# Reordering the opening of a one-core attention and gated-convolution kernel, with some of its steps on other engines

## The chip, the cores and the metric

The kernel runs on one core of one Trainium2 chip. The metric is device time in microseconds of one execution. Before the change the median of three runs was 580.38 us (580.14 to 581.49).

## What is computed

The reference is windowed attention with a linear distance bias, followed by a feed-forward block with a width-3 convolution as gate. Everything is float32.

```python
# attention: q, k, v are (8, 8, 576, 64); window 128
scores = scale * np.matmul(q, k.transpose(0, 1, 3, 2))
...
mask = (rel >= 0) & (rel < window)
scores = np.where(mask, scores + bias[None], -1000000000.0)
scores = scores - np.max(scores, axis=-1, keepdims=True)
attn = np.exp(scores)
attn = attn / (np.sum(attn, axis=-1, keepdims=True) + 1e-09)
return np.matmul(attn, v)
...
# feed-forward: x is (8, 576, 512), d_ff 1024, three taps along the sequence
h = np.maximum(x @ w_in, 0.0)
for k in range(K):
    conv_out += conv_w[k][None, None, :] * hp[:, k:k + S, :]
gate = 1.0 / (1.0 + np.exp(-conv_out))
return (h * gate) @ w_out
```

## The kernel before

The 8 x 576 tokens are 36 tiles of 128 (t = 0 to 35). Each tile's eight heads are handled as two halves u of four heads. The feed-forward block works on chunks of two tiles, in four steps of 256 hidden features each, so step s belongs to chunk s // 4. Most matmuls run on numbers that are split into a rounded high part and a low remainder, as three products: high by high, low by high, high by low.

The work is written as **pieces**. A piece is a name with numbers, and `emit` calls the function behind it; each engine runs its instructions in the order in which the pieces stand in three strings: `OPENING` (592 pieces: tiles 0 to 10, steps 0 to 10 in part, and the preparation of all weights), `PERIOD` (two tiles and four steps, repeated 14 times) and `TAIL`. An engine never overtakes: an instruction that waits holds up all that stand behind it on its engine, and on SP, which issues the DMAs, a DMA that waits for a free buffer holds up the next DMAs. The PSUM pool `pst` has five banks that are shared by all transposes, scores, attention products and up-projections.

The pieces that the text speaks of, with their engine:

- weights: `F` fetches block b (SP, L164; blocks 0 to 3 and 5 to 8 are w_in, 4 the taps, 9 to 16 w_out), `CL` clamps it (POOL, L171), `RP`/`RS` rescales its upper words (`w_rebias`: POOL L182 or ScalarE L184), `SG` keeps their sign alone (POOL, L188), `V` puts the bits together (DVE, two instructions, L203 or L207 and L210), `H` rounds to the high part (ACT, L216), `W` forms the low half (`w_lo`, L229: POOL for the blocks in `LOW_POOL`, else DVE).
- attention of tile t, half u: `QU` transposes q and k (PE, L324), `QV` copies them out (ACT, L330); from tile 9 on `TQ` (DVE, L342), `HQ` (ACT, L355) and `LQ` (POOL, L361) do this in their place; `S` scores (PE, L424, from tile 9 on L380), `MP` and `MB` mask and bias (DVE, L450 and L468), `X` exponentials (ACT, L476), `NR` reciprocals of the sums (L487 ACT, L488 DVE), `N` scales the rows by them (`normal`, L495: DVE for t < 8, else POOL) and `NA` the same on ACT in four instructions (`normal_act`, L501); `T` transposes (PE, L508), `RL` copies out (ACT, L513), `SEL` masks (POOL, L519 and L522), `AV` multiplies by v (PE, L626), `XH` and `XL` split the result into `ring`, the input of the feed-forward block (ACT L645, DVE L654), `XF` copies an edge (DVE, L660).
- feed-forward step s: `UH` up-projection (PE: L687 plain float32 for s < 4, L692 three products after), `HH` relu (ACT, L700 and L704), `Z` middle tap (ACT, L710), `CA` and `CB` outer taps (DVE, L725), `TH` tanh (ACT, L732), `GT` gate (DVE, L740), `GH` high part (ACT, L752), `GL` low half (`g_lo`, POOL, L760) and a copy of an edge (POOL, L761, or L756 for s < 4), `D` down-projection (PE, L784 for s < 4, L794 after), `OB` copies out and stores (ACT L810, then SP).

An up-projection of chunk 2 (`UH8`, `UH9`) needs `XL5` and `XL6`, which stand on DVE; a down-projection `D4` and later needs `GL` of its step and `W` of its two blocks.

Of the kernel before, what the change touches and what calls it, by code (L numbers as in the profile page):

```python
# [22 lines left out]
def tile_alibi_window_attention_conv_glu(  # L23
# [847 lines left out]
    X5.0.1 HH3.0 CA1.0 CB1.0 Z1.1 V12 XH3 XH4 CA1.1 UH3.1 QU7.1 NR5 NA5.1 T5.1 CB1.1 TH1 XL4 XL3 XF4 W3 W2 UH4.0
    UH5.0 QV7.1 GT1 RS9 SG9 Z2.0 LD9 HH2.1 QM7.1 RS11 HH3.1 CA2.0 CB2.0 Z2.1 KT6.0 X6.0.0 W6 RS13 UH4.1 CA2.1 HH4
    CB2.1 V9 S7.1 MP7.1.1 GL1 TH2 CL14 GT2 MP7.1.0 QU7.0 QV7.0 QM7.0 X6.0.1 SG13 Z3.0 X6.1.1 X6.1.0 CA3.0 LD12 CB3.0
    Z3.1 N6.0 UH5.1 D0 SG11 W7 UH7.0 RL5.1 T6.0 MB7.1.1 NA5.0 CL16 CA3.1 CB3.1 TH3 HH5 W10 T5.0 UH7.1 V11 GT3 RS16
    GL3 SEL5.1 RL5.0 MB7.1.0 H11 V13 Z4.0 CA4.0 S7.0 CB4.0 HH7 Z4.1 N6.1 MP7.0.0 GL2 CA4.1 SG16 MB7.0.0 SEL5.0 RL6.0
# [62 lines left out]
```

## Time and profile before

| | |
|---|---|
| median of three runs | 580.38 us (580.14 to 581.49) |
| profiled execution, its own time | 581.25 us |
| span of its instructions | 579.5 us |
| busy: PE, DVE, ACT, POOL | 562.4, 466.7, 434.2, 395.4 us |
| matmul instructions | 6121 |
| share of PE in the chain that ended last | 78% |

The profile is of one execution. A line's busy time is the time in which its instructions ran; "idle before" is the time in which the engine had nothing running just before them, with what ended it behind an arrow. The page's second part cuts the span into 40 slices of 14.5 us and gives the busy tenths of each engine and the clock that PE was granted. A busy PE is not PE at its peak, as matmuls are pipelined and their ends modelled; the distance from one group's start to the next one's says more.

### The profile page before, as it was taken

Reading aid. Unit: us, or ns where it says so; the run is one execution under the profiler, and the core shown is the slowest. Engines: PE = TensorE matmul, PEld = TensorE weight load, DVE = VectorE, ACT = ScalarE, POOL = GpSimd, SP = SyncE. Lnnn points to the kernel's source line nnn. Section 1 sums busy time; section 2 is a strip of 40 time slices with the busy share of each in tenths; the row PEclk is TensorE's granted clock in tenths of the full one; section 3 lists DMA queues with packets and bytes.
Section 4 is the critical chain, followed back from the end, with each engine's and each line's share of the span. In section 5 each row is a group of like instructions: output and inputs, shape, how many; then the busy total and the mean of one; then the engine's idle time right before and its main releaser. Section 6 shows DMA issues by size and latency. Waiting matters only on the chain.

```text
span 579.5 us, 16999 instructions
## 1 busy us (share of the span) xinstructions
PE 562.4 (97%) x6121; PEld 491.2 (85%) x6121; DVE 466.7 (81%) x1472; ACT 434.2 (75%) x1235; POOL 395.4 (68%) x451
## 2 busy tenths in 40 slices
PE   8898999799999999999999999999999999999997
PEld 7576886589898989898989898989898989899996
DVE  7798989898888987798778887788888987775444
...
PEclk9999999899999999999999999999999999999999
...
GB/s 191 259 228 198 138 98 57 42 108 124 167 128 162 123 162 132 158 137 161 134 162 131 164 133 170 127 172 122 171 121 168 126 166 82 146 110 18 21 3 73
DMA packets 141225, 76.63 MB, mean 132 GB/s; under 512 B 116412, under 2 KB 131028, under 8 KB 141140
## 3 DMA queue, kind: packets, MB, share of 16 engines
...
## 4 chain that ended last, share of the span: by engine, by line
PE 78%; DVE 10%; ACT 5%; DMA 2%; issue 2%; SPq 2%; POOL 1%; DVEq 0%; ACTq 0%; POOLq 0%
PE p L692 31%; PE o L794 31%; PE sc L380 7%; PE av L586 6%; DVE zp L725 2%; DVE sc L450 2%; DVE e L468 1%; ACT e L476 1%; DMA wst<-in_moe_w_in_dram 1%; DVE wg L210 1%; PE av L626 1%; SPq L164 1%; DMA rqk<-in_k_dram 1%; SPq L314 1%; DVE wst L203 1%
## 5 line engine op out<-in xcount | busy, mean ns | idle before, releaser
L692 PE MATMUL p<-ring,wi 128*128 128x256 f32 x1088 | 197.0, 283 | 3.0 <-DVE ring L654 3.0
L725 DVE SCALAR_TENSOR_TENSOR zp<-hh,cw,zp 128x256 f32<-128x256 f32 (+7 forms) x384 | 160.5, 418 | 41.3 <-ACT zp L710 34.2
L692 PEld LDWEIGHTS p<-ring,wi 128*128 128x128 f32 x1088 | 169.8, 189 | 7.4 <-issue 4.0
L692 PE MATMUL p<-ring,wl 128*128 128x256 f32 x544 | 152.9, 281 | 0.0
L760 POOL TENSOR_TENSOR gl<-z,gh 128x512 fp32r<-128x512 f32 x67 | 86.9, 1297 | 77.5 <-ACT gh L752 76.8
L476 ACT ACTIVATE e<-e,st 128x128 f32<-128x128 f32 x288 | 112.9, 394 | 18.3 <-DVE st L468 17.9
L794 PE MATMUL o<-wo,gh 128*128 128x512 f32 x270 | 110.3, 409 | 0.0
L794 PE MATMUL o<-wo,gl 128*128 128x512 f32 x270 | 105.8, 392 | 0.0
L794 PE MATMUL o<-wl,gh 128*128 128x512 f32 x270 | 105.6, 391 | 0.0
L692 PEld LDWEIGHTS p<-ring,wl 128*128 128x128 f32 x544 | 103.4, 190 | 0.0
L710 ACT ACTIVATE zp<-hh,cw 128x256 f32<-128x256 f32 x144 | 68.9, 479 | 30.4 <-DVE z L740 21.8
L361 POOL TENSOR_TENSOR qkT_low<-blk,qkT 128x1024 fp32r<-128x1024 f32 x27 | 65.1, 2411 | 16.9 <-ACT qkT L355 11.2
L495 POOL TENSOR_TENSOR e<-e,st 128x512 f32<-128x512 f32 x56 | 58.3, 1041 | 21.0 <-DVE st L488 20.1
L468 DVE CUSTOM_DVE_ANT_0 e<-sc,bias 128x128 f32<-128x128 f32 x288 | 69.2, 285 | 2.1 <-DVE sc L450 0.7
L732 ACT ACTIVATE zp<-zp 128x512 f32<-128x512 f32 (+1 forms) x73 | 42.1, 577 | 35.7 <-DVE zp L725 35.7
L794 PEld LDWEIGHTS o<-wo,gh 128*128 128x128 f32 x270 | 50.6, 187 | 13.7 <-issue 0.2
L794 PEld LDWEIGHTS o<-wo,gl 128*128 128x128 f32 x270 | 50.6, 187 | 12.0 <-POOL gl L760 0.4
L740 DVE SCALAR_TENSOR_TENSOR z<-zp,hh 128x512 f32<-128x512 f32 (+1 forms) x73 | 49.3, 675 | 13.5 <-ACT zp L732 11.6
L704 ACT ACTIVATE hh<-p 128x512 f32<-128x512 f32 x67 | 40.0, 597 | 25.2 <-PE p L692 25.0
L794 PEld LDWEIGHTS o<-wl,gh 128*128 128x128 f32 x270 | 50.8, 188 | 9.5
L450 DVE COPY_PREDICATED sc<-m_prev,sc 128x256 f32<-128x256 uint8 x128 | 51.1, 420 | 6.7 <-PE sc L380 6.7
L476 ACT ACTIVATION_READ_ACCUMULATOR e<-e,st 128x1 f32 x288 | 54.3, 189 | 0.0
...
## 6 DMA issues: line engine op xcount, KB each, us to landing
...
rr<-scr SPq DMA_DIRECT2D x112, 128.0 KB
...
rqk<-in_q_dram SPq DMA_DIRECT2D x216, 32.0 KB
rqk<-in_k_dram SPq DMA_DIRECT2D x216, 32.0 KB
...
```

The lines of the kernel that those rows point to most:

```text
L361: nc.gpsimd.tensor_tensor(out=turned_of(qkT_low, t), in0=blks[t], in1=hi, op=ALU.subtract)
L450: nc.vector.copy_predicated(out=s_cur, mask=mask.unsqueeze(1).to_broadcast(shp), data=data)
L468: nc.vector.tensor_tensor_reduce(out=e[:, j, :], in0=s_cur[:, g, :], in1=bias[:, head_of(t, u * HU + j), :], scale=-0.125, scalar=FAR, op0 ...
L476: nc.scalar.activation(out=e[:, j, :], in_=e[:, j, :], func=AF.Exp, bias=st[:, 0, j : j + 1], scale=-1.0, accum_out=st[:, 1, j : j + 1],)
L495: eng.tensor_tensor(out=e, in0=e, in1=st[:, 2, :].unsqueeze(2).to_broadcast([P, HU, P]), op=ALU.mult)
L692: nc.tensor.matmul(ps, a[:, part], ring[:, i, cc, cols], start=cc == 0 and n == 0, stop=cc == NCC - 1 and n == 2)
L710: nc.scalar.activation(out=zps[s][:, ff, :], in_=hhs[s][:, ff, 1 : 1 + CW], func=AF.Copy, scale=cw[:, 1, f : f + 1])
L725: nc.vector.scalar_tensor_tensor(out=z[:, ff, a:cut], in0=hh[:, ff, a + kk : cut + kk], scalar=cw[:, kk, f : f + 1], in1=z[:, ff, a:cut], ...
L732: nc.scalar.activation(out=zps[s][:, ff], in_=zps[s][:, ff], func=AF.Tanh)
L740: nc.vector.scalar_tensor_tensor(out=zgs[s][:, ff], in0=zps[s][:, ff], scalar=1.0, in1=hhs[s][:, ff, 1 : 1 + CW], op0=ALU.add, op1=ALU.mult,)
L760: nc.gpsimd.tensor_tensor(out=gl, in0=zgs.pop(s), in1=as32(gh), op=ALU.subtract)
L794: nc.tensor.matmul(to, a[:, ff, ms], w[:, part], start=first and n == 0, stop=end and n == 2)
```

## The change

Only the string `OPENING` and the rules for who does four kinds of step in it change. The first 54 pieces stay, some 100 more are nearly as before, and from piece 160 on the order is another one; the same pieces are done, each once. `PERIOD` and `TAIL` are as they were.

- Scaling the rows (`N`; `NA` is gone): (2,1) and (3,1) go from ACT to DVE, (6,0) from DVE to POOL, (7,0) and (7,1) from DVE to ACT.
- Low halves of the weights (`W`): 0, 1, 5 and 12 go from POOL to DVE, 6, 8 and 11 from DVE to POOL.
- Rescaling of the weights (`RS`; `RP` is gone): 3 and 8 go from POOL to ACT, 1, 7 and 11 from ACT to POOL.
- Low halves of the gate (`GL`): 4 and 7 go from POOL to DVE. The copies of the edge stay on POOL.

The two sets `KL_POOL` and `LQ_DVE` are empty.

```diff
-    LOW_POOL = {0, 1, 2, 3, 5, 7, 9, 10, 12, 13, 14, 15, 16}
+    LOW_POOL = {2, 3, 6, 7, 8, 9, 10, 11, 13, 14, 15, 16}
+    RB_POOL = {0, 1, 2, 5, 6, 7, 11}
+    N_ACT = {(1, 0), (2, 0), (3, 0), (4, 0), (4, 1), (5, 0), (5, 1), (7, 0), (7, 1)}
+    N_POOL = {(6, 0), (8, 0), (8, 1), (9, 0), (9, 1), (10, 0), (10, 1)}
+    GL_DVE = {4, 7}
+    KL_POOL = set()
+    LQ_DVE = set()
...
-    def w_rebias(b, pool=False):
+    def w_rebias(b):
...
-        if pool:
+        if b in RB_POOL:
             nc.gpsimd.tensor_scalar(out=g, in0=hf, scalar1=2.0**-112, scalar2=1.0, op0=ALU.mult, op1=ALU.mult)
...
-        eng = nc.vector if t < FIRST else nc.gpsimd
+        es[t, u] = e
+        if (t, u) in N_ACT:
+            for j in range(HU):
+                nc.scalar.activation(out=e[:, j, :], in_=e[:, j, :], func=AF.Copy, scale=st[:, 2, j : j + 1])
+            return
+        eng = nc.gpsimd if t > TURN + 1 or (t, u) in N_POOL else nc.vector
         eng.tensor_tensor(out=e, in0=e, in1=st[:, 2, :].unsqueeze(2).to_broadcast([P, HU, P]), op=ALU.mult)
...
-            nc.gpsimd.tensor_tensor(out=gl, in0=zgs.pop(s), in1=as32(gh), op=ALU.subtract)
+            eng = nc.vector if s in GL_DVE else nc.gpsimd
+            eng.tensor_tensor(out=gl, in0=zgs.pop(s), in1=as32(gh), op=ALU.subtract)
...
     OPENING = """
...
-    RS15 SG15 V15 W16 XL6 D2 HQ9 GH5 H12 Z6.0 MP8.0.0 LQ9 H15 CA6.0 GL5 CB6.0 MB8.0.0 LD10 X7.1.1 GH4 MP8.1.0 W13
...
+    MP8.1.0 TH5 GT5 D2 XH6 XL6 UH9.0 X8.0.0 MP8.1.1 Z6.0 CA6.0 CB6.0 GH4 H14 LD12 N7.0 T7.0 SG15 W10 W13 MP8.0.1 TQ9
+    W14 Z6.1 MB8.1.1 HQ9 UH8.0 V15 GH5 GL5 UH9.1 N7.1 CA6.1 CB6.1 TH6 UH8.1 H15 RL7.0 HH9 MB8.1.0 LD11 LV8 MB8.0.1
```

The order of the instructions shows the change at three places. (Line numbers of the changed kernel are 6 or so higher.) The first is DVE around `XL6`, the row that writes `ring` from `av6`, and `V15`, the two rows on `wst15` and `wg15`. Before:

```order
L654 TENSOR_TENSOR ring_126<-av5_1319,ring_126 128x4x128
L725 SCALAR_TENSOR_TENSOR zp5_1291<-hh1_132,cw_121,zp5_1291 128x256
L342 STREAM_TRANSPOSE blk_1390<-rqk9_1001 128x4x4x2x32
L740 SCALAR_TENSOR_TENSOR z5_1393<-zp5_1291,hh1_132 128x512
L203 SCALAR_TENSOR_TENSOR wst15_848<-wst15_848 128x512
L210 SCALAR_TENSOR_TENSOR wg15_1395<-wg15_1395,wst15_848 128x512
L654 TENSOR_TENSOR ring_126<-av6_1336,ring_126 128x4x128
```

Changed:

```order
L746 SCALAR_TENSOR_TENSOR z5_1394<-zp5_1293,hh1_132 128x512
L660 TENSOR_TENSOR ring_126<-av6_1326,ring_126 128x4x128
L458 COPY_PREDICATED sc8_1_1_1377<-m_prev_94,sc8_1_1_1377 128x2x128
L731 SCALAR_TENSOR_TENSOR zp6_1418<-hh2_133,cw_121,zp6_1418 128x256 x2
L496 RECIPROCAL st7_0_1213<-st7_0_1213 128x4
L458 COPY_PREDICATED sc8_0_1_1358<-m_prev_94,sc8_0_1_1358 128x2x128
L348 STREAM_TRANSPOSE blk_1460<-rqk9_890 128x4x4x2x32
L476 ISA e8_1_1390,st8_1_1391<-sc8_1_1_1377,bias_110 128x128
...
L209 SCALAR_TENSOR_TENSOR wst15_1033<-wst15_1033 128x512
L216 SCALAR_TENSOR_TENSOR wg15_1281<-wg15_1281,wst15_1033 128x512
```

`V15` and the transpose of tile 9 (`TQ9`) stood ahead of `XL6` and now stand behind it.

The second is ACT around `OB3`, the two copies to `ob0`, which wait for the down-projection `D3`, and the reciprocal sums of (8,0), the row that writes `st8_0` from itself. Before:

```order
L476 ACTIVATE e8_0_1414,st8_0_1415<-e8_0_1414,st8_0_1415 128x128 x2
L810 COPY ob0_0_1541<-o0_0_1124 128x512
L810 COPY ob0_1_1544<-o0_1_1125 128x512
L487 ACTIVATE st8_0_1415<-st8_0_1415 128x4
L710 ACTIVATE zp7_1522<-hh3_134,cw_121 128x256
```

Changed:

```order
L495 ACTIVATE st8_0_1372<-st8_0_1372 128x4
L716 ACTIVATE zp7_1552<-hh3_134,cw_121 128x256
L710 ACTIVATE hh0_131<-p8_1468 128x2x256
L817 COPY ob0_0_1632<-o0_0_1093 128x512
L817 COPY ob0_1_1635<-o0_1_1094 128x512
L758 CAST gh6_1638<-z6_1554 128x512
L738 ACTIVATE zp7_1552<-zp7_1552 128x512
```

The sums of (8,0) come ahead of the two copies; a high part and a tanh now stand behind them.

The third is DVE ahead of `V6`, the row that reads `wst6`, early in the opening. Before:

```order
L203 SCALAR_TENSOR_TENSOR wst10_420<-wst10_420 128x512
L210 SCALAR_TENSOR_TENSOR wg10_676<-wg10_676,wst10_420 128x512
L488 RECIPROCAL st4_501<-st4_501 128x8
L203 SCALAR_TENSOR_TENSOR low6_767<-wst6_465 128x512
L210 SCALAR_TENSOR_TENSOR wg6_742<-wg6_742,low6_767 128x512
```

Changed (the row of `V6` stands ten rows further down):

```order
L209 SCALAR_TENSOR_TENSOR wst10_420<-wst10_420 128x512
L216 SCALAR_TENSOR_TENSOR wg10_679<-wg10_679,wst10_420 128x512
L458 COPY_PREDICATED sc5_1_0_625<-m_prev_94,sc5_1_0_625 128x2x128
L458 COPY_PREDICATED sc5_1_0_625<-m_after_102,neg_90 128x2x128
L235 TENSOR_TENSOR wl5_725<-wg5_556,wi_119 128x512
L458 COPY_PREDICATED sc5_0_1_730<-m_prev_94,sc5_0_1_730 128x2x128
```

`W5` and one half of the mask and bias of (5,0) have come ahead of `V6`, as `W0`, `N2.1` and `N3.1` have further up.

## Rows read from the trace of the kernel before

**Rows 1.** The page's second part: busy tenths of PE and its granted clock.

```profile
PE   8898999799999999999999999999999999999997
...
PEclk9999999899999999999999999999999999999999
```

**Rows 2.** Windows: length, busy us of PE, PEld, DVE, ACT, POOL; clock, DMA, GB/s.

```profile
20.00:60.00 40.00, 35.80 (x261) 27.16 (x262) 35.95 (x119) 37.95 (x128) 31.76 (x43) 1.00 0.85 205
60.00:107.00 47.00, 41.49 (x344) 32.26 (x343) 43.54 (x96) 36.28 (x101) 28.49 (x33) 0.99 0.40 100
107.00:147.00 40.00, 39.26 (x367) 32.58 (x366) 33.05 (x111) 29.03 (x94) 27.09 (x31) 0.96 0.29 90
...
175.00:204.00 29.00, 29.00 (x369) 26.07 (x368) 26.79 (x89) 21.80 (x64) 21.92 (x25) 1.00 0.62 143
```

**Rows 3.** Waits from 20 to 147 us: who waited for whom, us, times, longest.

```profile
DVE st L488 <- ACT st L487: 7.0, 7, 2.8
...
PE p L692 <- DVE ring L654: 3.0, 1, 3.0
```

**Rows 4.** DVE in order of time, around XL6: start, us, what, idle before.

```profile
99.32 1.24 DVE L342 STREAM_TRANSPOSE blk<-rqk 128x1024 f32<-128x1024 f32 x1
...
101.40 1.75 DVE L203 SCALAR_TENSOR_TENSOR wst<-wst 128x512 uint32<-128x512 uint32 x1 [0.27 <-POOL wst L188]
103.25 2.64 DVE L210 SCALAR_TENSOR_TENSOR wg<-wg,wst 128x512 uint32<-128x512 uint32 x1
105.82 0.68 DVE L654 TENSOR_TENSOR ring<-av,ring 128x512 fp32r<-128x512 f32 x1
```

**Rows 5.** POOL in order of time in the same stretch.

```profile
102.56 2.79 POOL L361 TENSOR_TENSOR qkT_low<-blk,qkT 128x1024 fp32r<-128x1024 f32 x1
```

**Rows 6.** Windows of PE alone: length, busy us, granted clock, DMA.

```profile
105.00:106.00 1.00, 0.00 (x0) 1.00 0.29 65
...
107.00:108.00 1.00, 1.00 (x6) 0.50 0.33 73
```

**Rows 7.** The chain that ended last, in order of time: start, us, what.

```profile
40.65 6.17 DMA wst<-in_moe_w_in_dram
...
106.64 5.96 PE p L692 x36
...
151.81 5.69 PE p L692 x48
```

**Rows 8.** Single lines, 15 to 147 us: ns as shortest, median, longest.

```profile
L229 DVE TENSOR_TENSOR wl<-wg,wi x2: 686/1014/1341, 58.8 to 71.5; 128x512 fp32r<-128x512 f32 x2
L229 DVE TENSOR_TENSOR wl<-wg,wo x1: 1429/1429/1429, 118.5 to 118.5; 128x512 fp32r<-128x512 f32 x1
...
L495 DVE TENSOR_TENSOR e<-e,st x7: 684/693/1918, 14.5 to 120.9; 128x512 f32<-128x512 f32 x7
...
L760 POOL TENSOR_TENSOR gl<-z,gh x6: 1282/1292/1714, 105.3 to 142.3; 128x512 fp32r<-128x512 f32 x6
...
L501 ACT ACTIVATE e<-e,st x36: 385/394/414, 18.6 to 80.2; 128x128 f32<-128x128 f32 x36
```

**Rows 9.** DVE in order of time, early and late in the opening.

```profile
50.52 1.12 DVE L203 SCALAR_TENSOR_TENSOR low<-wst 128x512 uint32<-128x512 uint32 x1 [1.16 <-POOL wst L188]
...
116.79 0.18 DVE L488 RECIPROCAL st<-st 128x4 f32<-128x4 f32 x1 [2.81 <-ACT st L487]
...
120.92 1.92 DVE L495 TENSOR_TENSOR e<-e,st 128x512 f32<-128x512 f32 x1
```

**Rows 10.** ACT in order of time: the second of the two copies of OB3.

```profile
116.07 0.59 ACT L810 COPY ob<-o 128x512 f32<-128x512 f32 x1 [1.13 <-PE o L784]
```

**Rows 11.** PE in order of time: AV6, the first scores of tile 9 and of tile 11.

```profile
96.55 1.09 PE L626 MATMUL av<-rl,rv 128*64 128x128 f32 x16 [0.35 <-POOL rl L522]
...
117.83 0.33 PE L380 MATMUL sc<-qkT 32*128 32x128 f32 x4
...
147.16 0.38 PE L380 MATMUL sc<-qkT 32*128 32x256 f32 x1 [0.82 <-DVE ring L654]
```

More of the change, by code (lines that the diff above doesn't have):

```diff
@@ L871, in tile_alibi_window_attention_conv_glu @@
[L871 to L875, printed above, removed]
@@ L876, in tile_alibi_window_attention_conv_glu @@
-    UH6.0 RS14 H9 UH6.1 HH6 Q8 W9 CB4.1 SEL6.0 X7.0.0 SH14 V14 TH4 GT4 V16 H14 W14 Z5.0 CA5.0 MP7.0.1 QO8 CB5.0 T6.1
-    RL6.1 SEL6.1 QL8 H13 Z5.1 CA5.1 H16 D1 MB7.0.1 AV5 AV6 XH5 X7.1.0 XL5 S8.1 XH6 S8.0 CL15 LV7 CB5.1 TQ9 TH5 GT5
-    RS15 SG15 V15 W16 XL6 D2 HQ9 GH5 H12 Z6.0 MP8.0.0 LQ9 H15 CA6.0 GL5 CB6.0 MB8.0.0 LD10 X7.1.1 GH4 MP8.1.0 W13
-    MP8.0.1 Z6.1 UH9.0 W12 UH9.1 X7.0.1 UH8.0 CA6.1 D3 CB6.1 TH6 N7.0 T7.0 X8.0.0 LV9 GT6 MB8.1.0 MB8.0.1 HH9 Z7.0
-    CA7.0 UH8.1 MP8.1.1 CB7.0 X8.0.1 OB3 N8.0 MB8.1.1 TQ10 W11 Z7.1 CA7.1 CB7.1 RL7.0 N7.1 GL4 S9.0 TE8.0 HQ10 LQ10
@@ L881, in tile_alibi_window_attention_conv_glu @@
[L881 to L884 removed]
+    X0.0.0 RS0 MP0.1.0 MB0.1.0 QU1.1 QV1.0 I2 S1.0 SG0 F3 QV1.1 MP0.1.1 MB0.1.1 X0.0.1 MP1.0.1 MB1.0.1 I2 S1.1 I2
@@ new lines, in tile_alibi_window_attention_conv_glu @@
+    X5.1.0 HH0.1 LD7 MP5.0.0 MB5.0.0 UH2.0 QV6.1 UH3.0 KH6.1 KL6.1 Z0.0 CA0.0 RL4.1 SEL3.0 MP6.0.0 CB0.0 S6.1 CL12
+    SEL4.0 H3 SEL3.1 AV3 MP6.0.1 H2 RS12 SG12 Z0.1 MB6.0.0 X5.0.0 SEL4.1 AV4 W1 HH2.0 CA0.1 CB0.1 MP6.1.0 CL9 MB6.1.0
+    KL6.0 MB6.0.1 HH3.0 X5.0.1 H7 LD9 TH0 NR5 GT0 XH3 X6.1.0 V12 Z1.0 CA1.0 CB1.0 UH3.1 GL0 XH4 UH2.1 XL4 F13 KT6.0
+    RS9 MP6.1.1 N5.1 XL3 W2 Z1.1 CA1.1 CB1.1 XF4 H6 SG9 HH3.1 H8 MB6.1.1 TH1 GT1 QU7.1 QV7.1 W3 QU7.0 QM7.1 Z2.0
+    HH2.1 CA2.0 T5.1 CB2.0 W8 RL5.1 CL11 RS11 KT6.1 SG11 F16 V9 CL13 Z2.1 CA2.1 CB2.1 UH4.0 CL16 X6.1.1 X6.0.0 QV7.0
@@ new lines, in tile_alibi_window_attention_conv_glu @@
+    MP8.1.0 TH5 GT5 D2 XH6 XL6 UH9.0 X8.0.0 MP8.1.1 Z6.0 CA6.0 CB6.0 GH4 H14 LD12 N7.0 T7.0 SG15 W10 W13 MP8.0.1 TQ9
+    W14 Z6.1 MB8.1.1 HQ9 UH8.0 V15 GH5 GL5 UH9.1 N7.1 CA6.1 CB6.1 TH6 UH8.1 H15 RL7.0 HH9 MB8.1.0 LD11 LV8 MB8.0.1
+    X8.0.1 TQ10 Z7.0 GT6 X8.1.0 LQ9 D3 CA7.0 CB7.0 W16 GL4 N8.0 Z7.1 HH8 W12 CA7.1 S9.0 MP9.1.0 OB3 GH6 GL6 CB7.1 TH7
+    MP9.1.1 MB9.1.1 X8.1.1 GT7 MP9.0.1 TE8.0 T7.1 RL7.1 MB9.0.1 Z8.0 N8.1 CA8.0 CB8.0 HQ10 LQ10 MP9.0.0 Z8.1 W15
+    SEL7.0 TE8.1 WE8 X9.0.1 D4 D5 D6 CA8.1 CB8.1 TH8 GT8 GH7 SEL7.1 MB9.0.0 X9.0.0 MB9.1.0 GL7 N9.0 UH10.1 Z9.0 CA9.0
@@ L885, in tile_alibi_window_attention_conv_glu @@
+    GH8 GL8 CB9.0 S10.0 D7 MP10.1.0 MB10.1.0 MP10.1.1 X9.1.0 MB10.1.1 X9.1.1 N9.1 Z9.1 X10.1.0 X10.1.1 TE9.0 SE8
+    CE8.1 CA9.1 CB9.1 TH9 MP10.0.0 GT9 UH10.0 N10.1 CE8.0 TE9.1 MP10.0.1 LV9 WE9 OB7
     """
```

49 lines of the change are left out of this document (21 added, 28 removed).

## The prediction, made before the changed kernel ran

> **What bounds the kernel now.** I began with the slices of the page [rows 1]. PE shows sevens and eights in the first eight slices (116 us) and nines after them, and its clock is granted in full but for a slice or two there. The windows say the same in microseconds [rows 2]: in the period PE is busy 29.00 of 29.00, and the nines go on to the tail. As the period and the tail keep their order, time can be won or lost only by when PE gets through the opening. There it is busy 35.80 of 40, 41.49 of 47 and 39.26 of 40 us [rows 2]: 10.4 us idle, of which the middle window has most.
>
> DVE is the engine beside it. It is busy 35.95, 43.54 and 33.05 us in the three windows [rows 2], so 14.5 us idle, and the list of waits puts 7.0 us of that down to reciprocals that wait for a sum from ACT [rows 3]. The longest wait of PE itself is one of 3.0 us, an up-projection that waits for a row of `ring`, a DVE instruction [rows 3].
>
> The order of time shows why. XL6, 0.68 us, starts at 105.82, directly behind the two instructions of V15, which ran 1.75 and 2.64 us [rows 4]. Other such instructions take 0.69 us when nothing stands against them (W on DVE, same size, shortest 686 ns) [rows 8]. Beside V15 POOL ran LQ9, from 102.56 for 2.79 us [rows 5]. So V15 cost 4.39 where 1.38 would do. PE stood still meanwhile, and when it went on its granted clock was 0.50, the lower of its two levels (1.2 of 2.4 GHz) [rows 6]. The 36 matmuls that came then took 5.96 us; 48 at full clock take 5.69, so 36 would take 4.27 [rows 7]. That is 1.7 us on top of the 3.0.
>
> At the very end of the opening PE waits again for DVE, 0.82 us before the scores of tile 11 [rows 11]. So neither engine leads by much, and I keep an account for each. The later of the two sets the time.
>
> **The change in PE's account.** XL6 now stands in front of V15 and TQ9 (first pair of order rows). Its wait of 3.0 goes, and with it the 1.7 at the low clock: -4.7 us. What is late next is the down-projection D2 ahead of it on PE, so nothing more comes of it. The select that held AV6 for 0.35 [rows 11] stands earlier on POOL: -0.35.
>
> Against this, V6 comes later on DVE. In front of it now stand N2.1, N3.1, W0 and W5, 0.69 each [rows 8], 2.8 us, and half of the mask and bias of (5,0), which is then missing further down and so makes no difference at XF4, where UH4 waits. V6 waited 1.16 us for POOL [rows 9], which swallows part. What POOL waited for was block 6, 6.17 us on its way after V5 gave a buffer free [rows 7]; V5 is late by the first three of these, 2.1, so block 6 lands later too, but V6 is later by more. What is left at XF4 is 2.8 - 1.2 = +1.6 (between V6 and XF4 W8 leaves DVE and W1 comes). Its ends are 0, if PE has slack there, and 2.8.
>
> PE: -4.7 - 0.35 + 1.6 = **-3.5 us**.
>
> **The change in DVE's account.** By the sets, DVE loses one N and gains one W and two GL, net two instructions of 0.69: +1.4. (GL on DVE is not in the trace; W has the same operands, two from SBUF and one float32r out, so I take 0.69, and 1.43, W's longest [rows 8], as the upper end.)
>
> V15 no longer meets LQ9, whose input TQ9 and HQ9 make later; POOL has W10, W13, W14 there. Free it would save 3.0; if both halves take 1.43, as W11 did, 1.5. I take 1.5, since POOL's queue is not empty there.
>
> N7.1 took 1.92 [rows 9], W11 1.43 and W8 1.34 [rows 8]; all three leave DVE, and what they took over 0.69 is 1.2 + 0.7 + 0.7 = 2.6. New on DVE are N2.1, N3.1, W0, W1, W5, W12, GL4 and GL7. The ten N and W of the trace were stretched by these 2.6 in all, 0.26 each; eight times that is 2.1. Net -0.5.
>
> N8.0's reciprocal waited 2.81 us on DVE [rows 9]: its sum stood on ACT behind the two copies of OB3, the second of which ran at 116.07 after waiting for PE [rows 10]. Now the sum is ahead of them (second pair of order rows). But a tanh is now behind them, and DVE soon needs the scores of tile 9, which PE makes after the same D3. I take half, 1.4, between 0 and 2.8. And V6's 1.16 goes: -1.2.
>
> DVE: +1.4 - 1.5 - 0.5 - 1.4 - 1.2 = **-3.2 us**.
>
> The other moves cost nothing by these rows. Two N (7,0 and 7,1) add 4 x 0.39 us each on ACT [rows 8], as two (2,1 and 3,1) leave it. ACT loses one rescaling. POOL gets it and one N for two GL of 1.29 [rows 8] and one W, and is idle 8 to 18 us in each window [rows 2]. On SP, F13 now stands behind the 16 issues of LD9, and LV9 behind SE8; block 13 is wanted by D6 and v of tile 9 in the period, and the DMA share of the last two windows is 0.40 and 0.29 [rows 2], so neither is late by these rows. If ACT's cover were gone, T7.0 would wait for N7.0, at most its 1.6 us.
>
> The smaller gain rules: -3.2. The profiled execution took 581.25 us (579.5 of span and 1.75 around it) and would take 578.05. It lies 0.87 above the median of the runs shown, so I forecast 580.38 - 3.2 = **577.2 us**.
>
> **A rule that speaks against it.** The trace shows one DVE instruction of V15 at 2.64 us with LQ9 beside it, and N and W between 0.69 and 1.92 [rows 4, 5, 8]. The Trainium skill, page "SBUF — State Buffer", section "Who interferes with whom", says that a DVE instruction with two SBUF inputs and a GpSimd instruction that reads SBUF exclude each other, the later one blocked until the first has ended. These rows agree with it, and by it each of the eight instructions new on DVE is exposed. If each stood behind a whole instruction like GL, 1.29 [rows 8], they would lose 10.3 us, and DVE's sum would be +5.0; by the mean of the rows it is -3.2.
>
> **The rivals.**
>
> *Slower: the moved instructions are blocked by POOL.* Place: GL4 and W12 beside LQ9, W16 and the N of tile 8; W0, W1, W5 beside the selects and weights of the first 60 us. Price: if each of the eight loses what N7.1 lost, 1.23, DVE has 9.8 in place of 2.1: -3.2 + 7.7 = +4.5, **584.9 us**; at 1.0 each 583. It decides from 0.66 each on, where the gain is gone. For it speaks V15; against it that most of the old ones ran nearly free: N's shortest is 684 ns and its median 693 [rows 8]. Chance 0.22.
>
> *No change: the wait moves to the scores of tile 9.* LQ9 ended at 105.35 and these scores began at 117.83 [rows 5, 11], 12.5 us of cover. Now TQ9 (1.24) [rows 4], a copy on ACT, GL5 (1.29) [rows 8] and LQ9 (2.79) come one after another behind XL6, some 6 us, and three W on POOL, taken like GL, may come between: up to 10. PE has two up-projections (48 matmuls, 5.69 [rows 7]) and D3, which has no row here, to cover it. If POOL is 2 to 3 us late, PE idles again, and the low clock with its 1.7 can come again: 577.2 + 1.5 + 1.7 = **580.4 us**. Chance 0.21.
>
> *More: both accounts at their good ends.* Without the early lag PE has -4.7 - 0.35, and without the 0.82 wait at the end -5.9; DVE would allow it (V15 free, the whole 2.81 saved: -6.1). **574.5 us**. Chance 0.12.
>
> **How the numbers follow.** The forecast, between 574.5 and 578.6, has 0.45. A measurement of this kernel can tell some 0.3%, 1.74 us, from no change: faster is below 578.6, slower above 582.1. Faster is then 0.45 + 0.12 = 0.57, same 0.21, slower 0.22. The range reaches from a microsecond below the good end, 573.5, to the slower case at 1.0 us each, 583.
>
> **What would show it.** Right: no PE wait for `ring` of 3 us near 100 to 107 us and no window of that stretch at 0.50; V15 below 3 us in all; N8.0's reciprocal waiting less than 1.5; the scores of tile 11 some 3 us ahead of 147.16 [rows 11]. V6 should start near 53 us in place of 50.52 [rows 9]. Wrong: GL or W on DVE above 1.3 us as a rule; a PE wait before the scores of tile 9 or before T7.0; a PE idle stretch of 2 us or more ahead of UH2, with a low clock behind it. If PE reaches the period earlier but then waits in it for DVE, the gain of PE's account was there and DVE's was not.

## The result, and the profile after

The changed kernel took **571.36 us** (median of 4 runs, 570.92 to 573.09) beside 580.39 for the kernel before on the same chip. The ratio is 0.9846, 95% interval 0.9823 to 0.987: 9.0 us faster, where 3.2 were forecast and the range ended at 573.5. The direction was right and the size was not. The profiled execution took 570.92 us, with a span of 569.2. (PE is TensorE, DVE is VectorE, ACT is ScalarE, POOL is GpSimd, SP is SyncE.)

The page's slices of the changed kernel, which answer to [rows 1]:

```profile
PE   8889999999999999999999999999999999999997
...
PEclk9999999999999999999999999999999999999999
```

PE's nines now begin with the fourth slice, and the slice with the lower clock is gone. The windows (columns as in [rows 2]) say how much:

```profile
20.00:60.00 40.00, 36.31 (x313) 28.88 (x313) 38.57 (x131) 37.20 (x128) 28.50 (x40) 1.00 0.92 221
60.00:107.00 47.00, 45.47 (x345) 36.21 (x340) 43.76 (x107) 41.16 (x117) 34.20 (x39) 1.00 0.33 83
107.00:147.00 40.00, 40.00 (x456) 34.52 (x459) 36.02 (x125) 31.05 (x96) 29.27 (x32) 1.00 0.49 136
175.00:204.00 29.00, 29.00 (x374) 26.06 (x372) 27.54 (x93) 23.02 (x67) 23.12 (x26) 1.00 0.57 141
```

In the three windows of the opening PE idles 5.2 us in place of 10.4 [rows 2], and the middle one gave most of it: 5.5 became 1.5. DVE idles 8.7 in place of 14.5. The clock of the second and third window is 1.00 in place of 0.99 and 0.96, by these shares some 2 us of PE's time. The windows are cut at fixed times: the third holds 11 us of the period in the changed kernel, and in those PE has no idle time. The period keeps its 29.00 of 29.00.

The list of waits from 20 to 147 us, where [rows 3] stood (who waited for whom: us, times, longest):

```profile
DVE z L746 <- ACT zp L738: 2.0, 4, 0.7
DVE zp L731 <- ACT zp L716: 1.9, 5, 1.0
...
PE p L698 <- DVE st L476: 1.3, 2, 1.0
```

The 7.0 us of reciprocals and the 3.0 us of PE's wait for `ring` are gone from the list, down to waits of 0.6 us. In their place stand small waits for tanh and for the middle tap. DVE in order of time, around XL6 and V15 (answers to [rows 4, 9]):

```profile
96.75 0.68 DVE L660 TENSOR_TENSOR ring<-av,ring 128x512 fp32r<-128x512 f32 x1
...
99.00 1.23 DVE L348 STREAM_TRANSPOSE blk<-rqk 128x1024 f32<-128x1024 f32 x1
...
100.55 0.68 DVE L209 SCALAR_TENSOR_TENSOR wst<-wst 128x512 uint32<-128x512 uint32 x1
101.27 0.70 DVE L216 SCALAR_TENSOR_TENSOR wg<-wg,wst 128x512 uint32<-128x512 uint32 x1
...
108.26 0.17 DVE L496 RECIPROCAL st<-st 128x4 f32<-128x4 f32 x1
```

XL6 comes at 96.75 in place of 105.82. V15 takes 1.38 in all, the free time, in place of 4.39. N8.0's reciprocal, the last row, has no idle time before it. POOL beside it (answers to [rows 5]):

```profile
102.02 1.30 POOL L767 TENSOR_TENSOR gl<-z,gh 128x512 fp32r<-128x512 f32 x1 [2.19 <-DVE wg L216]
103.25 0.20 POOL L768 COPY hh<-hh 128x4 f32<-128x4 f32 x1
103.39 2.41 POOL L368 TENSOR_TENSOR qkT_low<-blk,qkT 128x1024 fp32r<-128x1024 f32 x1
```

POOL stood still while V15 ran. GL5 waited 2.19 us, by the profile for the end of V15 (101.97); the high part that it reads (GH5 on ACT) ended only at 101.94, so it could hardly have come sooner. LQ9 followed. PE in order of time, UH9 behind XL6, the first scores of tile 9 and those of tile 11 (answers to [rows 6, 11]):

```profile
98.11 0.80 PE L698 MATMUL p<-ring,wi 128*128 128x256 f32 x2
...
108.63 0.33 PE L387 MATMUL sc<-qkT 32*128 32x128 f32 x4
...
135.54 0.39 PE L387 MATMUL sc<-qkT 32*128 32x256 f32 x4
```

UH9 starts 8.5 us earlier than before (106.64, [rows 7]). For the scores of tile 11, the row at 147.16 [rows 11] is their fourth matmul, behind the wait of 0.82; the first three ran ahead of it:

```profile
145.84 0.50 PE L380 MATMUL sc<-qkT 32*128 32x256 f32 x3
```

So they start 10.3 us earlier, and the lead is 11.6 us behind that wait. At the end of the span 10.3 are left; 0.76 of what is lost is one wait of PE in the period of this execution (425.77). Some 1.4 us of the lead lie ahead of everything that changed: the second reciprocals waited 2.59 us in the profiled execution before and 1.30 in this one. They started at 18.34 and 16.92, and in e1 and e13 to e15, whose pieces up to there are those of before, between 16.93 and 17.39.

From 20 us to the start of these scores PE is idle 5.2 us in place of 9.8, and busy 110.3 in place of 116.1 with nearly the same matmuls. The low clock accounts for some 1.7 of the latter. The other 4 us are matmuls that follow each other more closely in many places; no single wait holds them.

### The profile page after: what moved, and what is told of

It reads as the page before. It is cut to its first block, busy times and chain, and to the rows that moved or that the text cites. A ratio compares the mean times of both kernels' runs of the same rounds, so it can differ in the third digit from the quotient of the medians.

```text
span 569.2 us, 16993 instructions
## 1 busy us (share of the span) xinstructions
PE 557.9 (98%) x6121; PEld 489.8 (86%) x6121; DVE 462.3 (81%) x1474; ACT 433.4 (76%) x1234; POOL 394.4 (69%) x450
## 4 chain that ended last, share of the span: by engine, by line
PE 82%; DVE 9%; ACT 4%; DMA 2%; issue 2%; POOL 1%; SPq 0%; DVEq 0%; ACTq 0%
PE o L801 34%; PE p L698 31%; PE sc L387 8%; PE av L592 6%; DVE sc L458 2%; DVE e L476 1%; DMA rqk<-in_k_dram 1%; DVE zp L731 1%; DVE wg L216 1%; ACT e L484 1%; PE sc L432 1%; DVE wst L209 1%; DVE low L209 1%; PE o L791 1%; DVE e L508 1%
## 5 line engine op out<-in xcount | busy, mean ns | idle before, releaser
L767 POOL TENSOR_TENSOR gl<-z,gh 128x512 fp32r<-128x512 f32 x65 | 83.9, 1290 | 65.7 <-ACT gh L758 60.0
L508 POOL TENSOR_TENSOR e<-e,st 128x512 f32<-128x512 f32 x57 | 59.8, 1049 | 23.9 <-DVE st L496 23.6
L801 PEld LDWEIGHTS o<-wo,gl 128*128 128x128 f32 x270 | 50.6, 187 | 11.6
```

Source lines behind the costliest of these rows:

```text
L767: eng.tensor_tensor(out=gl, in0=zgs.pop(s), in1=as32(gh), op=ALU.subtract)
L801: nc.tensor.matmul(to, a[:, ff, ms], w[:, part], start=first and n == 0, stop=end and n == 2)
```

## The experiments

Eighteen kernels ran. A ratio is to the kernel before on the same chip, with its 95% interval in brackets.

| experiment | us | ratio |
|---|---|---|
| e1 before, XL6 ahead of V15 | 578.10 | 0.9955 [0.9940, 0.9971] |
| e2 changed, V15 ahead of XL6 | 573.36 | 0.9869 [0.9835, 0.9903] |
| e3 changed order, old engines | 580.97 | 1.0016 [0.9993, 1.0040] |
| e4 old order, new engines | 587.31 | 1.0109 [1.0079, 1.0138] |
| e5 changed, old rescalings | 577.82 | 0.9952 [0.9932, 0.9973] |
| e6 changed, old W | 570.47 | 0.9834 [0.9811, 0.9857] |
| e7 changed, old N | 575.60 | 0.9917 [0.9890, 0.9943] |
| e8 changed, old GL | 571.45 | 0.9850 [0.9826, 0.9873] |
| e9 change up to UH4.0 alone | 579.16 | 0.9975 [0.9956, 0.9993] |
| e10 change up to AV6 alone | 574.24 | 0.9895 [0.9865, 0.9925] |
| e11 changed, N8.0 behind OB3 | 572.29 | 0.9851 [0.9818, 0.9884] |
| e12 changed, old W and GL | 572.69 | 0.9868 [0.9839, 0.9896] |
| e13 before, LQ9 later | 579.40 | 0.9969 [0.9948, 0.9990] |
| e14 before, N8.0 ahead of OB3 | 578.29 | 0.9972 [0.9958, 0.9987] |
| e15 before, three reciprocals later | 580.61 | 1.0000 [0.9985, 1.0016] |
| e16 changed, N7.0 and N7.1 on DVE | 572.61 | 0.9874 [0.9851, 0.9897] |
| e17 change behind AV6 alone | 579.28 | 0.9984 [0.9970, 0.9998] |
| e18 change from UH4.0 to AV6 alone | 576.37 | 0.9933 [0.9912, 0.9954] |

### Order or engines (e1 to e4)

Two theories stood at first. By theory A the order does it, with XL6 ahead of V15 as its core; by theory B that swap is nearly all there is. e3 and e4 then part the change along its other seam.

**e1**, the swap alone in the kernel before:

```diff
-    RS15 SG15 V15 W16 XL6 D2 HQ9 GH5 H12 Z6.0 MP8.0.0 LQ9
+    RS15 SG15 XL6 V15 W16 D2 HQ9 GH5 H12 Z6.0 MP8.0.0 LQ9
```

> The kernel before with one swap on DVE: XL6 ahead of V15, nothing else. Theory A (DVE is the bound of the whole opening, and the gain is DVE time that was idle or blocked, some 9 us of it): the swap frees no DVE time beyond what V15 loses beside LQ9, so most of PE's 3.0 us wait and the low clock go, but PE meets DVE again before the period: 579 to 580.4 us, a gain of 0 to 1.5. Theory B (the one PE wait with its low clock is a term of its own, 4.7 us, and the rest came from somewhere else): 575.5 to 577.5 us.

578.10 us, 2.6 less: more than A said and less than B. **e2**, the swap undone in the changed kernel:

```diff
-    MP8.1.0 TH5 GT5 D2 XH6 XL6 UH9.0 X8.0.0 MP8.1.1 Z6.0 CA6.0 CB6.0 GH4 H14 LD12 N7.0 T7.0 SG15 W10 W13 MP8.0.1 TQ9
-    W14 Z6.1 MB8.1.1 HQ9 UH8.0 V15 GH5 GL5 UH9.1 N7.1
+    MP8.1.0 TH5 GT5 D2 XH6 SG15 V15 XL6 UH9.0 X8.0.0 MP8.1.1 Z6.0 CA6.0 CB6.0 GH4 H14 LD12 N7.0 T7.0 W10 W13 MP8.0.1 TQ9
+    W14 Z6.1 MB8.1.1 HQ9 UH8.0 GH5 GL5 UH9.1 N7.1
```

> The changed kernel with SG15 and V15 put back ahead of XL6. Theory A: DVE has the same work in all; V15 is 1.4 us when free, and PE waits that much for XL6 at most and makes part of it good: 571.4 to 573. Theory B: the wait and the low clock come back, 3 to 4.7 us: 574.5 to 576.

573.36, a little above theory A's bound and below theory B's. It is more than the changed kernel by 1.3 (by the ratios) or 2.0 (by the medians), but the intervals overlap, so a loss isn't shown. The changed kernel without the swap is 7 us faster than the kernel before: the swap is a part, and not the largest.

What the swap did not mend in e1 is V15 itself. DVE of e1 in order of time:

```profile
100.13 0.67 DVE L654 TENSOR_TENSOR ring<-av,ring 128x512 fp32r<-128x512 f32 x1
100.72 1.51 DVE L203 SCALAR_TENSOR_TENSOR wst<-wst 128x512 uint32<-128x512 uint32 x1
102.34 2.69 DVE L210 SCALAR_TENSOR_TENSOR wg<-wg,wst 128x512 uint32<-128x512 uint32 x1
```

XL6 is out of the way, but V15 still takes 4.2 us and holds up what follows on DVE.

**e3**, the changed order with all engines as before, and **e4**, the order of before with the new engines:

```diff
-    LOW_POOL = {2, 3, 6, 7, 8, 9, 10, 11, 13, 14, 15, 16}
-    RB_POOL = {0, 1, 2, 5, 6, 7, 11}
-    N_ACT = {(1, 0), (2, 0), (3, 0), (4, 0), (4, 1), (5, 0), (5, 1), (7, 0), (7, 1)}
-    N_POOL = {(6, 0), (8, 0), (8, 1), (9, 0), (9, 1), (10, 0), (10, 1)}
-    GL_DVE = {4, 7}
+    LOW_POOL = {0, 1, 2, 3, 5, 7, 9, 10, 12, 13, 14, 15, 16}
+    RB_POOL = {0, 2, 3, 5, 6, 8}
+    N_ACT = {(1, 0), (2, 0), (2, 1), (3, 0), (3, 1), (4, 0), (4, 1), (5, 0), (5, 1)}
+    N_POOL = {(8, 0), (8, 1), (9, 0), (9, 1), (10, 0), (10, 1)}
+    GL_DVE = set()
```

(e3; e4 has the `-` lines in the kernel before.)

> The changed order, with N, W, RS and GL on the engines of the kernel before. Theory A, with the order as the cause: most of the gain stays, 571 to 575 us. Theory C (the gain is mainly from the steps that left DVE, N7.0 and N7.1 above all, and from GL and W at other places): most of it goes, 577 to 580 us.

> The order before, with N, W, RS and GL on the engines of the changed kernel. Theory A: no gain to speak of, 578 to 583 us, as the reciprocals wait as before and the eight new instructions on DVE meet POOL at unplanned places. Theory C: 573 to 577 us.

580.97 and 587.31, both above every bound that was set for them. Neither half brings anything alone; the engines alone cost 6.3 us by the ratio. Theory A, by which the order alone pays, fell here, and so did its counterpart. What an order is worth depends on who does the steps in it. e5 to e8 ask which steps; e5 and e7 below lose 6.2 and 4.1 us by the ratios, which together is about the 9.9 that e3 lacks.

### Which engines the order needs (e5 to e8, e12, e16)

Each takes one line of the sets of e3 back in the changed kernel (e12 two lines, e16 a part of one).

**e5:**

```diff
-    RB_POOL = {0, 1, 2, 5, 6, 7, 11}
+    RB_POOL = {0, 2, 3, 5, 6, 8}
```

> The changed kernel with the old table for the rescales alone (1, 7 and 11 on ACT; 3 and 8 on POOL). Theory P (the engine table matters at a few places of the new order, where the wrong engine waits with a queue behind it): with the old table RS1 stands in ACT's queue ahead of the step that NR0 needs, and its piece of weights has not landed; in the run with all old engines ACT idled 5.30 us before it and DVE 5.12 us before NR0. So 574.5 to 577.5, and both waits are seen here again. Theory S (only the work and the stretch on DVE count): no DVE instruction moves, so 570.5 to 572.

577.82, 6 us more: theory P, at its upper end. Where they go is seen on ACT in order of time, and on DVE in the second fence:

```profile
18.13 0.66 ACT L190 ACTIVATE wg<-wst 128x512 f32<-128x512 f32 x1 [4.59 <-POOL wst L177]
18.70 0.19 ACT L495 ACTIVATE st<-st 128x8 f32<-128x8 f32 x1
```

```profile
18.92 0.20 DVE L496 RECIPROCAL st<-st 128x8 f32<-128x8 f32 x1 [4.38 <-ACT st L495]
```

RS1 needs a clamped block that has just landed. In the new order it stands ahead of the sum of the first reciprocals; on ACT it keeps that sum waiting, and DVE with it. On POOL it stands behind the clamp that it needs anyway, and nobody waits. In e5 PE waits 3.65 us for a copy of q and k on ACT, and its granted clock is 0.50 from 18 to 22 us and 0.67 from 22 to 26. In the order of before RS1 stands behind the sums of the first two reciprocals, where it can't hold them up. So its place on POOL is a condition for the new order; what it is worth in the old one was not run alone.

**e7:**

```diff
-    N_ACT = {(1, 0), (2, 0), (3, 0), (4, 0), (4, 1), (5, 0), (5, 1), (7, 0), (7, 1)}
-    N_POOL = {(6, 0), (8, 0), (8, 1), (9, 0), (9, 1), (10, 0), (10, 1)}
+    N_ACT = {(1, 0), (2, 0), (2, 1), (3, 0), (3, 1), (4, 0), (4, 1), (5, 0), (5, 1)}
+    N_POOL = {(8, 0), (8, 1), (9, 0), (9, 1), (10, 0), (10, 1)}
```

> The changed kernel with the old table for the scalings alone (6.0, 7.0, 7.1 back to DVE; 2.1, 3.1 to ACT). Theory P: N7.0 and N7.1 stand beside POOL's blocks again and took 1.59 and 1.56 us in the run with all old engines, N3.1 on ACT waited there 1.84 us for DVE: 573 to 576. Theory S: DVE has one scaling more, 0.69 us, and some 1.8 us of stretch: 572.5 to 574.

575.60, some 4.1 more: theory P. **e16** takes back N7.0 and N7.1 alone:

```diff
-    N_ACT = {(1, 0), (2, 0), (3, 0), (4, 0), (4, 1), (5, 0), (5, 1), (7, 0), (7, 1)}
+    N_ACT = {(1, 0), (2, 0), (3, 0), (4, 0), (4, 1), (5, 0), (5, 1)}
```

> The changed kernel with N7.0 and N7.1 on DVE and all else as in it. Of the 4.2 us that all the old scalings cost, theory N7 (two products of 1.57 and 1.55 us on DVE beside POOL's blocks): 573.5 to 575.5. Theory N3 (N3.1 on ACT behind a wait of 1.7 us, with MP5.1.1 and NR4 waiting on DVE behind it): 571 to 572.5.

572.61, a little above theory N3's bound: 1.2 to 1.6 of the 4.1, with an interval that overlaps the changed kernel's, though both products took 1.57 and 1.56 us on DVE beside POOL. Where the rest of the 4.1 comes from is not shown. One candidate is N3.1, where ACT waits for DVE and, behind it, DVE for ACT; this half was not run alone. Another is the clock: in e7 PE waits 1.32 us at 104.64 and from 106 to 108 us its granted clock is 0.50, some 1.7 us by the shares around it; in e16 the wait is the same, 1.32 at 102.78, and the clock stays at 1.00. ACT and DVE of e7 at N3.1, in order of time:

```profile
35.50 0.99 ACT L505 ACTIVATE e<-e,st 128x128 f32<-128x128 f32 x3 [1.71 <-DVE st L496]
```

```profile
40.35 0.43 DVE L458 COPY_PREDICATED sc<-m_prev,sc 128x256 f32<-128x256 uint8 x1 [1.98 <-ACT x_first L650]
```

**e6**, **e8** and **e12**:

```diff
-    LOW_POOL = {2, 3, 6, 7, 8, 9, 10, 11, 13, 14, 15, 16}
+    LOW_POOL = {0, 1, 2, 3, 5, 7, 9, 10, 12, 13, 14, 15, 16}
...
-    GL_DVE = {4, 7}
+    GL_DVE = set()
```

(e6 the first pair, e8 the second, e12 both.)

> The changed kernel with the old table for the low halves alone (0, 1, 5, 12 back to POOL; 6, 8, 11 to DVE). Theory P: the pieces are spread over the opening and only W1, W12 and W11 feed something close behind; POOL gets one more 1.28 us subtraction and N8.0's product or LQ9 follow later: 571.5 to 574. Theory S: DVE loses one 0.69 us subtraction net, but meets POOL more often (W11 and W8 took 1.43 and 1.34 us on DVE before): 570.5 to 572.

> The changed kernel with the low halves of the gate 4 and 7 back on POOL. Theory P: POOL idles for short stretches there, but GL4's place follows LQ9 and N8.0's product comes behind it, so up to 1 us later for S9: 571 to 573. Theory S: DVE loses 0.68 and 1.17 us: 569.5 to 571.

> The changed kernel with the low halves of weights and gates all as before, the scalings and rescalings new. If only RS and N need their new engines: 569.5 to 571.5, with 3 subtractions fewer on DVE (2.1 us of its work) that bring at most 1 us, since TensorE is busy 98% there. If the low halves matter as a pair: 573 to 575.

570.47, 571.45 and 572.69: none can be told from the changed kernel. By the bounds e6 is a hair below theory S, e8 lies within theory P, e12 between its two cases. Nine of the moved steps, and 2.1 us of DVE's work, make no measurable difference.

### Where in the opening the gain arises (e9, e10, e17, e18)

The pieces ahead of a chosen place, or behind it, stand in the new order on the new engines, all others as before. In e9 the seam lies behind UH4.0, in e10 behind AV6 (the diffs show the order around the seam against that of the changed kernel; the engines follow the same seam):

```diff
     KT6.1 SG11 F16 V9 CL13 Z2.1 CA2.1 CB2.1 UH4.0
-    CL16 X6.1.1 X6.0.0 QV7.0 UH4.1 F15 N6.1 TH2 GT2 UH5.0 UH5.1 S7.1
+    LV6 H10 LV8 F15 UH5.0 X6.0.0 W6 RS13 UH4.1 HH4 S7.1 MP7.1.1 GL1
...
```

```diff
     CA5.0 MB7.0.0 X7.0.0 AV5 V14 H13 LV6 SEL6.1 AV6
-    CB5.0 QO8 QL8 H16 XH5 XL5 HH7 Z5.1 W11 CA5.1 CB5.1 S8.0
+    LV8 LD12 W10 HH7 H14 W14 QO8 CB5.0 QL8 Z5.1 CA5.1 H16 XH5
...
```

> The change up to UH4.0 alone: up to that piece the order and the engines of the changed kernel, behind it the rest in the order and on the engines of before. Theory L (the gain arises late, from XL6 on; the up-projection UH4.0 starts only 0.7 us earlier in the changed kernel's trace once the 1.4 us of an earlier start are taken off): 578.5 to 580.5. Theory F (the new order has filled DVE's idle time early: at UH4.0 it has issued 21 pieces more and 4 fewer than before, with CA2, CB2, GT1 and V9 some 4 us of DVE work, and this lead is cashed in later): 574.5 to 577.

> The change up to AV6 alone, behind it the rest as before, with V15 ahead of XL6, N8.0 behind OB3 and N7.0, N7.1 on DVE. Theory L: AV5 is 2.1 us earlier once the start is taken off, so 577 to 579; the 8 us that are left arise behind it. Theory F: the lead is kept and some of the late waits go with it: 573.5 to 576.

579.16 and 574.24: theory L for the first seam, theory F for the second. By the ratios the part up to UH4.0 brings 1.5 us, up to AV6 6.1 in all, and what lies behind AV6 the remaining 2.9. In e9 V15 takes 1.75 and 2.64 as before. In e10, with V15 still ahead of XL6, it is free. DVE of e10 in order of time, and POOL beside it:

```profile
99.11 0.67 DVE L209 SCALAR_TENSOR_TENSOR wst<-wst 128x512 uint32<-128x512 uint32 x1
99.81 0.70 DVE L216 SCALAR_TENSOR_TENSOR wg<-wg,wst 128x512 uint32<-128x512 uint32 x1
100.44 0.67 DVE L660 TENSOR_TENSOR ring<-av,ring 128x512 fp32r<-128x512 f32 x1
```

```profile
99.82 2.94 POOL L368 TENSOR_TENSOR qkT_low<-blk,qkT 128x1024 fp32r<-128x1024 f32 x1 [2.25 <-ACT qkT L361]
```

This time LQ9 began 0.01 us behind V15's second half and not 0.69 ahead of it [rows 4, 5], and it is LQ9 that is stretched, 2.94 in place of 2.41.

**e17** makes the part behind AV6 alone, **e18** the part between (against the kernel before):

```diff
     Z5.1 CA5.1 H16 D1 MB7.0.1 AV5 AV6
-    XH5 X7.1.0 XL5 S8.1 XH6 S8.0 CL15 LV7 CB5.1 TQ9 TH5 GT5
+    CL15 LD10 X7.1.1 X7.0.1 LV7 RS15 X7.1.0 H12 XH5 XL5 W11 CB5.1 S8.0
...
```

```diff
     T5.1 CB1.1 TH1 XL4 XL3 XF4 W3 W2 UH4.0
-    UH5.0 QV7.1 GT1 RS9 SG9 Z2.0 LD9 HH2.1 QM7.1 RS11
+    LD9 X6.1.0 KT6.0 RS9 SG9 HH3.1 GT1 QV7.1 QU7.0 QM7.1 Z2.0 HH2.1 CA2.0
...
+    H12 CA5.0 MB7.0.0 X7.0.0 AV5 V14 H13 SEL6.1 AV6
     LD12 W10 HH7 H14 W14 QO8 CB5.0 QL8 Z5.1 CA5.1 H16 XH5 XL5
```

> The change behind AV6 alone: up to that piece the order and engines of before, behind it those of the changed kernel. If the parts add: 577 to 578.5. If the late part removes the wait of XL6 and the low clock by itself (as the swap alone did, 2.6 us) and then the reciprocals' waits and the slow W11 and N7.1 too: 573 to 576.5.

> The change between UH4.0 and AV6 alone: before it and behind it the order and engines of before. If the parts add: 575 to 576.5, with V15 free of LQ9 and no low clock at 107. If the middle part needs the lead that the first part gives DVE: 577.5 to 580, with V15 again over 3 us or another wait in its place.

e18 brings 3.9 us by itself, which its interval (2.7 to 5.1) does not tell from the 4.6 of a sum, with V15 at 0.67 and 0.70 and no wait of PE above 0.9. As in e10, LQ9 begins 0.01 us behind V15's second half (101.31 and 101.30) and takes 2.94. e17 brings 0.9, less than either bound foresaw, and less than the 2.6 of the swap alone. Its V15 is free too, 0.70 and 0.69. But the wait has only moved one step forward, to XL5, and PE waits for that row of `ring` as long as it did for the other. DVE of e17 in order of time, and PE's row in its list of waits:

```profile
100.67 0.69 DVE L660 TENSOR_TENSOR ring<-av,ring 128x512 fp32r<-128x512 f32 x1 [3.04 <-ACT ring L651]
```

```profile
PE sc L432 <- DVE ring L660: 3.4, 1, 3.4
```

So the late part brings 2.9 with the other two and next to nothing alone in this cut. That it needs the middle for more than the cut itself isn't shown: X7.1.1, X7.0.1, RS15, X7.1.0 and H12, which the new order does ahead of AV6, stand on ACT in front of XH5 in e17, which starts at 100.06 directly behind them, and that is enough to make XL5 late.

### The terms of the sum, one by one (e11, e13 to e15)

**e13** takes LQ9 away from V15 in the kernel before and leaves XL6 where it was:

```diff
-    RS15 SG15 V15 W16 XL6 D2 HQ9 GH5 H12 Z6.0 MP8.0.0 LQ9 H15 CA6.0 GL5 CB6.0 MB8.0.0 LD10 X7.1.1 GH4 MP8.1.0 W13
-    MP8.0.1
+    RS15 SG15 V15 W16 XL6 D2 HQ9 GH5 H12 Z6.0 MP8.0.0 H15 CA6.0 GL5 CB6.0 MB8.0.0 LD10 X7.1.1 GH4 MP8.1.0 W13 LQ9
+    MP8.0.1
```

> The kernel before with POOL's LQ9 moved behind W13, so that it no longer runs beside V15; XL6 stays behind V15 and TQ9. Theory K (the collision is the whole of the wait and what hangs on it): V15 in 1.4 to 2.8 us in place of 4.39, TensorE's wait for ring at most 1.5 in place of 3.0, no low clock at 107, D3 and OB3 earlier and with them N8.0's wait shorter: 575.5 to 578. Rival (order of XL6 matters, not the collision; GL5 comes beside V15 instead): 579.5 to 581.

579.40, 1.8 less by ratio. GL5 came beside V15 in LQ9's place. DVE of e13 in order of time:

```profile
100.68 1.74 DVE L203 SCALAR_TENSOR_TENSOR wst<-wst 128x512 uint32<-128x512 uint32 x1 [0.26 <-POOL wst L188]
102.53 1.56 DVE L210 SCALAR_TENSOR_TENSOR wg<-wg,wst 128x512 uint32<-128x512 uint32 x1
```

V15 is 1.1 us shorter and PE's wait falls by the same 1.1, from 3.0 to 1.9. The size lies between the two bounds. The first half of V15 is as long as before, 1.74, since what ran beside it from its start was W16 and not LQ9, here from 100.60 for 1.27 us and before at the same place:

```profile
101.33 1.27 POOL L229 TENSOR_TENSOR wl<-wg,wo 128x512 fp32r<-128x512 f32 x1
```

**e14** and **e11** move N8.0 and nothing else:

```diff
-    X8.0.1 OB3 N8.0 MB8.1.1 TQ10 W11
+    X8.0.1 N8.0 OB3 MB8.1.1 TQ10 W11
```

```diff
-    W16 GL4 N8.0 Z7.1 HH8 W12 CA7.1 S9.0 MP9.1.0 OB3 GH6
+    W16 GL4 Z7.1 HH8 W12 CA7.1 S9.0 MP9.1.0 OB3 N8.0 GH6
```

(e14 in the kernel before, e11 in the changed one.)

> The kernel before with N8.0 ahead of OB3, nothing else. The prediction's reading (the sum stands on ACT behind OB3): the 2.81 us wait goes and half of it or more shows in the time: 577.6 to 579. Theory K (the wait hangs on the late D3, and what follows it needs D3's engine time anyway; TensorE has work to cover): 579.5 to 581, with DVE waiting a little later for something else.

> The changed kernel with N8.0 put back behind the two parts of OB3. The prediction's reading (ACT's sum for N8.0 stands behind OB3, and the reciprocal waits for it): half of the 2.81 us wait comes back, 572.5 to 574. The rival (the wait came from DVE being early there and is filled by the pieces that are now around it): 571 to 572.

e14 brings 1.6 us (0.8 to 2.4), as the prediction read it: the 2.81 us wait is gone and about half of it shows. e11 loses nothing that can be measured, as its rival said; in the changed kernel N8.0 does not wait even behind OB3, since D3, and so OB3, is no longer late. Nor does it wait much in e1, where it also stands behind OB3: from 100 us on no reciprocal waits longer than 0.8 us there.

**e15** moves the other reciprocals:

```diff
-    Z3.1 N6.0 UH5.1 D0 SG11 W7 UH7.0 RL5.1 T6.0 MB7.1.1 NA5.0
+    Z3.1 UH5.1 D0 SG11 W7 UH7.0 RL5.1 MB7.1.1 N6.0 T6.0 NA5.0
...
-    Z4.1 N6.1 MP7.0.0 GL2 CA4.1 SG16
+    Z4.1 MP7.0.0 GL2 CA4.1 N6.1 SG16
...
-    TH6 N7.0 T7.0 X8.0.0 LV9 GT6 MB8.1.0 MB8.0.1 HH9
+    TH6 X8.0.0 LV9 GT6 MB8.1.0 MB8.0.1 N7.0 T7.0 HH9
```

> The kernel before with N6.0, N6.1 and N7.0 one to three DVE steps later each (their transposes behind them), so that DVE does ready work where it idled 1.06, 0.67 and 0.76 us. If idle DVE time in the opening counts in full: 577.5 to 578.5. If DVE's waits there are covered by others that follow: 579.5 to 581.

580.61, ratio 1.0000. Two of the three waits went, N6.0 still waited 1.05, and GT6 now waited 0.72. These waits of DVE are covered by others; that the prediction gave them nothing was right.

## Why the prediction was wrong in size

The step that failed is the account of DVE and the rule "the smaller gain rules", which made it the forecast. It counted DVE's time one for one, and it knew two of DVE's waits, V6's and half of N8.0's, 2.6 us together. In the traces DVE's idle time from 20 us to the row of `ring` ahead of the scores of tile 11 (146.41 before, 134.71 in the changed kernel) falls from 14.5 to 7.8 us, and its busy time from 111.9 to 106.9. Its place was wrong too. The steps that were to bring the gain (XL6, V15, N8.0, W11, N7.1) stand behind AV6; by the runs 1.5 us arise up to UH4.0, 4.6 between it and AV6, where the sum of PE had 0.35, and 2.9 behind AV6.

**What bounds the kernel.** Right: the gain lies in the opening, the two waits of [rows 3] are gone, and PE is as busy in the period as before.

**PE's account, XL6, -4.7.** The wait and the low clock behind it are gone, as I said, but I tied them to one edit and took their price too high. The swap alone brings 2.6 (e1), not 4.7. Most of that can be the clock: against the executions of the kernel before whose mean clock was not low (median 578.88, and 579.66 on e1's chip) e1 is 0.8 to 1.6 us faster. So the 3.0 us of idle time were made good in large part elsewhere. The middle part alone, in which XL6 still stands behind V15, brings 3.9 (e18); there V15 no longer waits for LQ9, and what else that part brings is not told apart. In the changed order the swap is worth nothing that can be told from noise (e2).

**V15 beside LQ9.** I put all of the 3.0 us over its free 1.38 down to LQ9. That holds for the second half of V15, 1.95 us; the first half, 1.06, was W16's (e13). In the changed order both are out of the way.

**PE's account, +1.6 at XF4.** Wrong in sign. V6 came 1.1 us later in e9 (51.59 in place of 50.52), where I had 2.8 ahead of its wait, and XF4 1.8 us earlier (67.08 and 68.84). I put N2.1, N3.1, W0 and W5 on the path to V6, though the window from 20 to 60 us had 4 us of idle DVE [rows 2] to take them: DVE is busy 38.57 there now, in place of 35.95. And I took the half of mask and bias of (5,0) that is missing behind V6 for no difference; by the starts of the rows it is 1.3 us less between V6 and XF4, and MB6.1.1, now behind XF4, another 0.4. UH4 started 0.6 earlier in e9, not 1.6 later; it waits 1.02 us there, by the profile for that MB6.1.1. The part up to it gains 1.5 us where I charged 1.6.

**DVE's account, -3.2, which set the forecast.** V6's wait of 1.16 is gone, as I had it. The other terms:

- Two more instructions, +1.4: not seen in the time. e12 takes three instructions off DVE again, 2.1 us, and is no faster.
- V15: I took half, 1.5, since I expected POOL not to be empty beside it. It runs free, 1.38, so the term is -3.0.
- The stretch: the eight new instructions take 0.80 and 0.70 (N2.1, N3.1), 0.72, 1.18, 0.68 and 0.66 (W0, W1, W5, W12), 0.68 and 1.17 (GL4, GL7), 1.1 us over 0.69 each, where I had 2.1. But N6.1, which stayed on DVE and which I left out, took 1.81 (at 71.98), the longest of the next row. Over all N, W and GL on DVE the stretch is 2.4 us in place of 2.7: net -0.3, close to my -0.5.

```profile
L508 DVE TENSOR_TENSOR e<-e,st x6: 686/749/1811, 14.3 to 72.0; 128x512 f32<-128x512 f32 x6
```

- N8.0: the whole 2.81 went, not half. In the kernel before half is right for the edit I named (e14); the late D3, which I had not counted as a third cost of the collision, beside the wait and the clock, makes this wait too: it is at most 0.8 in e1, without that edit.

With the sizes measured the account is +1.4 - 3.0 - 0.3 - 2.8 - 1.2 = -5.9, and PE's, even with its 4.7 left as it was and the 0.6 of UH4 in place of the +1.6, is -4.7 - 0.35 - 0.6 = -5.7. Neither reaches 9.0, and neither is more than a sum: e12 and e15 move DVE's work and waits by 1 to 2 us and the time stays. The 3 us beyond them are not traced to steps. One part is seen: the 0.82 wait ahead of the last scores of tile 11, which my case with more had, is still there in e10 (0.8) and gone in the changed kernel. What the rest is stays open.

**The rivals.** The slower case fell: the eight moved instructions lost 1.1 us, not 9.8. The case of no change fell too, and less widely: LQ9 ended at 105.80 and the scores of tile 9 began at 108.63, so of 12.5 us of cover 2.8 were left, as that rival had feared, and they were enough. The case with more, 574.5, was nearest and still 3 us short.

**What would show it.** No wait for `ring`, no window at 0.50, V15 below 3 and N8.0 below 1.5 all came. V6 near 53 did not (50.05), and the scores of tile 11 were 11.6 us ahead of the row named (10.3 from first to first), not 3.

**Engines.** I had costed the rescalings at nothing and the two N on ACT likewise. The changed kernel shows no wait for them, and yet taking the rescalings back costs 6 us (e5). A price of nothing for a step meant "nothing, in this order".
